# RWKV5 attention and an MLP-Mixer layer: `r` of 14 units is loaded with four consecutive tokens of two heads per partition

## The chip, the cores and the metric

The kernel runs on one core of one Trainium2 chip. The metric is the device time of one execution in microseconds; the number given for a kernel is the median of its runs.

## What is computed

Four sequences of 768 tokens, 8 heads of 48 channels. The attention keeps one 48 x 48 state per head, which decays by `w` per token:

```python
for t in range(S):
    kt, vt, rt = (k[:, :, t], v[:, :, t], r[:, :, t])
    cur = np.einsum('bhd,bhe->bhde', u[None] * kt, vt)
    y[:, :, t] = np.einsum('bhd,bhde->bhe', rt, state + cur)
    state = w[None, :, :, None] * state + np.einsum('bhd,bhe->bhde', kt, vt)
```

Its output, with the heads side by side as 384 channels, goes through a mixer layer. The token half mixes along the sequence, the channel half along the channels:

```python
xt = x.transpose(0, 2, 1)
h = np.maximum(xt @ w_tok1, 0.0) @ w_tok2
u = x + h.transpose(0, 2, 1)
h2 = np.maximum(u @ w_ch1, 0.0) @ w_ch2
return (u + h2)
```

All inputs and the output are float32 in DRAM; `r`, `k` and `v` are stored as (batch, head, token, channel), so 48 floats (192 bytes) of one head and token are contiguous, and so are consecutive tokens of one head.

## The kernel before

The 24 units of work are 4 batches times 6 chunks of 128 tokens, in that order. For each unit SyncE (SP) loads `k`, `r` and `v` into tiles `ld_k`, `ld_r`, `ld_v` of 128 partitions (one token each) by 8 heads by 48 channels. `lpool` holds eight units, so a load of unit u+8 waits until unit u has used its tile. The decay over time is taken out by products: `kp` multiplies `k` by a table `wn`, `rp` multiplies `r` by a table `wp`; both are powers of `w`, made at the start by ScalarE (ACT) as exp(t ln w), with t from `iota` and one table for each of G = 3 chunk positions. ln w comes from `w_ps`, in which a matmul of a column of ones has copied `w` to all partitions. The products go in bf16 to `kpr`, with each head padded to 64 columns, so that two heads fill 128.

`kpr` must then be turned, channels on partitions. For units 0 to 13 TensorE (PE) does it (`trk`, `trr`, into `tr_ps` in PSUM), and ACT copies the result to SBUF as `rk` (one copy of 1024 columns, or for the units in `rk_two` a copy of 512 for `k` and one for `r`: `rkk`, `rkr`). Units 14 to 23 (`turned`) are turned by a DMA transpose, `turn_unit`. From `rk` come the scores (`at_ps`), which VectorE (DVE) masks to `AT`; `y` adds the unit's own part and, through the state `S`, that of the units before; `yd` is the part of `u`; `x_b` is the attention's output. The mixer follows for each batch: `hid` (`wtok1`), `hr`, `bk` (`wtok2`), `us` (`u_sb`), `uT` (turned), then `z` (`wch1`), `zr`, `h` (`wch2`) and `os`, which is stored.

The order on each engine is fixed when the program is built. `graph` lists all steps with the engines that they may run on, their times and a rank; `Plan.run` simulates this and gives the order, and `InOrder` keeps it. The change doesn't touch `graph` or its numbers. Parts of it that the prediction speaks of:

- SP issues all loads and stores in one order, `transfers` at line 416, with a store or a transpose between them where it falls due. POOL (GpSimd) does most `kp` and `rp` products and issues the six weight transfers behind some of them (`wafter`, line 436): the two `wtok` after its products of unit 4, the four `wch` (two halves of `wch1`, two halves of `wch2`) after those of unit 5.
- `hold` lets the load of `k` for unit 6 wait until `y` of unit 5 is done.
- TensorE turns, scores and mixes in this one order too; while it waits early on, `fill` gives it idle matmuls.

Of the kernel before, what the change touches and what calls it, by code (L numbers as in the profile page):

```python
# [13 lines left out]
f32 = mybir.dt.float32  # L14
bf16 = mybir.dt.bfloat16
i32 = mybir.dt.int32
# [3 lines left out]
Exp = ACTF.Exp  # L20
Ln = ACTF.Ln

B, H, S, D = 4, 8, 768, 48
T = 128
C = S // T
G = C // 2
HP = H // 2
NJ = 12
NU = B * C
LEAD = 4  # L30
NLOAD = 8
LATER = tuple(range(2 * C, NU))

# [134 lines left out]
def graph(do, cfg):  # L168
# [49 lines left out]
    for u in range(NU):  # L218
# [4 lines left out]
        t_at, t_y, t_yS = cfg.get("pe_times", ((0.36, 0.25, 0.185),) * 2)[u >= C]  # L223
        old = xs.get(u - LEAD)
        d = cfg.get("dve_late", {}).get("kr", 0.5) if u >= cfg.get("early", 6) else cfg.get("kr0", 0.5)
# [189 lines left out]
CFG = dict(apart=2.0,   # L415
    transfers=[("u", u) for u in range(0, 6)]
    + [('k', 6)]
    + [('r', 6)]
    + [('k', 7)]
    + [('r', 7)]  # L420
    + [('v', 6)]
    + [('v', 7)]
    + [('u', 8)]
# [31 lines left out]
    late={'kp2': -0.6},  # L455
    hold={6: ('y', 5), 21: ('us', '2_2')},
    by_pe=range(0, 14),
    turned=range(14, 24),
    warm=(2, 4),
    fill_from=16.5,  # L460
# [5 lines left out]
def kernel(  # L466
# [13 lines left out]
    nc = tc.nc  # L480
    assert tuple(r.shape) == (B, H, S, D)
    dm = H * D
    MID = G * T // 2
# [2 lines left out]
    dch = moe_w_ch1.shape[1]  # L486
    by_pe = CFG.get("by_pe", range(NU))
    direct = CFG.get("direct", ())

    const = ctx.enter_context(tc.tile_pool(name="const", bufs=1))  # L490
    wts = ctx.enter_context(tc.tile_pool(name="wts", bufs=1))
    lpool = ctx.enter_context(tc.tile_pool(name="lpool", bufs=NLOAD))
    apool = ctx.enter_context(tc.tile_pool(name="apool", bufs=LEAD + 1))
    xpool = ctx.enter_context(tc.tile_pool(name="xpool", bufs=1))
# [3 lines left out]
    psM = ctx.enter_context(tc.tile_pool(name="psM", bufs=4, space=bass.MemoryType.PSUM))  # L498
# [19 lines left out]
    pe, dve, act, pool, sp = (InOrder(e) for e in (nc.tensor, nc.vector, nc.scalar, nc.gpsimd, nc.sync))  # L518
    ENG = {"PE": pe, "DVE": dve, "ACT": act, "POOL": pool, "SP": sp}

    def h3(t):
        return t.rearrange("p (h d) -> p h d", h=H)
# [2 lines left out]
    idle = const.tile([128, 512], bf16, name="idle")  # L525
    dve.memset(idle, 0.0)
    row = const.tile([1, dm], f32, name="row")
    rows = const.tile([2 * HP, 2, P], f32, name="rows")
    dve.memset(rows, 1.0)
    wide = len(by_pe) < NU  # L530
    u_bc = const.tile([128, dm], f32, name="u_bc") if wide else None
    act.dma_start(out=row, in_=w.rearrange("h d -> (h d)")[None, :])
    act.preload_act_table_set("natural_log_exp_and_others")
    ones = const.tile([1, 128], f32, name="ones")
    dve.memset(ones, 1.0)


    idle_ps = psM.tile([128, 512], f32, name="idle_ps", tag="m")
    w_ps = psM.tile([128, dm], f32, name="w_ps", tag="m")

    def warm(n):
        for _ in range(n):
            pe.matmul(idle_ps, idle[:, 0:128], idle, start=True, stop=True)

    warm(CFG.get("warm", (1, 10))[0])
    pe.matmul(w_ps, ones, row, start=True, stop=True)
    warm(CFG.get("warm", (1, 10))[1])

    iota_i = const.tile([128, 2, G], i32, name="iota_i")
# [1 line left out]
    pool.iota(iota_i[:, 1, :], pattern=[[-T, G]], base=MID - 1, channel_multiplier=-1)  # L551
    iota = const.tile([128, 2, G], f32, name="iota")
    dve.tensor_copy(iota, iota_i)
    ident = const.tile([128, 128], bf16, name="ident")
    make_identity(nc, ident)
    mask = const.tile([128, 128], f32, name="mask")
    pool.memset(mask, 1.0)
    pool.affine_select(
        out=mask, in_=mask, compare_op=ALU.is_gt,
# [12 lines left out]

    NB = LEAD + 1
    kprs = []
    for i in range(NB):
        t = const.tile([128, 2, H, P], bf16, name=f"kpr{i}")
# [16 lines left out]
    lnw = const.tile([128, dm], f32, name="lnw")  # L593
    wn = const.tile([128, G, dm], f32, name="wn")
    wp = const.tile([128, G, dm], f32, name="wp")
    wu_sb = const.tile([128, 2, HP], f32, name="wu_sb")
    wG = const.tile([128, HP], f32, name="wG")
    wGm = const.tile([128, HP, 2, D], f32, name="wGm")

    def lnw_(eng):  # L600
        act.activation(lnw, w_ps, Ln)

    def wn_(eng, g):
        act.activation(wn[:, g, :], lnw, Exp, scale=iota[:, 1, g:g + 1])

    def wp_(eng, g):
        act.activation(wp[:, g, :], lnw, Exp, scale=iota[:, 0, g:g + 1])

    def wu(eng):
# [20 lines left out]
    SRC = {"k": k, "r": r, "v": v}  # L630
    loaded, L, Z, M = {}, [dict() for _ in range(NU)], {}, [dict() for _ in range(B)]
    kvs, INS, M0 = [None, None], {}, {}

    def load(eng, nm, i):
        b, c = divmod(i, C)
        t = lpool.tile([128, dm], f32, name=f"ld_{nm}")
        ins = sp.dma_start(h3(t), SRC[nm][b, :, ts(c, T), :].rearrange("h s d -> s h d"))
        if i in CFG.get("hold", {}) and nm == "k":
            first = INS["".join(map(str, CFG["hold"][i]))]
            tc.add_manual_dep(ins.ins, first.ins.name,  # L640
                              mybir.DependencyInfo(mybir.DependencyClass.Sync, mybir.DependencyReason.DATA),
                              reason="weights first")
        loaded[nm, i] = t
# [15 lines left out]
        ENG[eng].tensor_mul(kprs[i % NB][:, 0, :, 0:D], h3(loaded["k", i]), h3(wn[:, i % G, :]))  # L659

    def rp(eng, i):
        ENG[eng].tensor_mul(kprs[i % NB][:, 1, :, 0:D], h3(loaded["r", i]), h3(wp[:, i % G, :]))

    def vb(eng, i):
        L[i]["vb"] = apool.tile([128, dm], bf16, name="vb")
        INS[f"vb{i}"] = act.copy(L[i]["vb"], loaded["v", i])

# [12 lines left out]
    def yd(eng, i):  # L680
        L[i]["yd"] = apool.tile([128, dm], f32, name="yd", bufs=LEAD)
        ENG[eng].tensor_mul(h3(L[i]["yd"]), h3(L[i]["vb"]), L[i]["adg"].unsqueeze(2).to_broadcast([128, H, D]))
# [12 lines left out]

    def rk(eng, i):
        L[i]["rk"] = apool.tile([128, 2, HP, T], bf16, name="rk")
        (act.copy if eng == "ACT" else dve.tensor_copy)(L[i]["rk"], L[i]["tr"])

    def rkp(eng, i, j):  # L700
        if "rk" not in L[i]:
            L[i]["rk"] = apool.tile([128, 2, HP, T], bf16, name="rk")
        (act.copy if eng == "ACT" else dve.tensor_copy)(L[i]["rk"][:, j], L[i]["tr"][:, j])

    def atq(eng, i, q):
        if q == 0:
# [20 lines left out]
    def AT(eng, i, q):  # L727
        if q is None:
# [267 lines left out]
```

## Time and profile before

| | |
|---|---|
| median of 3 runs | 166.17 us (164.99 to 168.54) |
| profiled execution, first to last instruction | 166.5 us |
| its own time, as given | the span is all that is given for it, 0.3 us above the median |
| TensorE matmul busy | 156.8 us (94%) |
| DVE, ACT, POOL busy | 106.8, 87.2, 65.3 us |
| read from and written to DRAM | 20.65 and 4.72 MB |
| DMA packets | 97427, of which 90753 under 512 bytes |

Times in the profile's rows count from the span's start, in us; a row of the timeline has start, duration, engine, line and operation, with output, inputs and shape, then the idle time ahead of it and what ended that. All engine instructions pass through one helper, so they show line L512 and are told apart by their tiles. "SPq" and "POOLq" are the issuing of DMAs. q1 is SP's queue, q10 ACT's, q0 POOL's.

### The profile page before, as it was taken

What the parts mean: (1) busy time and instruction counts of PE and PEld (TensorE: products, weight loads), DVE (VectorE), ACT (ScalarE), POOL (GpSimd) and SP (SyncE); (2) the same over time, 40 slices, a digit from 0 to 9 for tenths busy, and PEclk for the clock granted to TensorE, in tenths of its full rate; (3) what the DMA queues carried; (4) which work ended last, traced back from release to release, by engine and by line L of the source; (5) the groups of instructions that cost most, each with busy time, mean ns of one, the idle gap of its engine ahead of it and who ended that gap; (6) DMA issues with size and microseconds to landing.
All of it is one profiled execution on the core that took longest, in us unless ns stands there. A gap on an engine that the chain in (4) does not pass through costs nothing.

```text
span 166.5 us, 3791 instructions
## 1 busy us (share of the span) xinstructions
PE 156.8 (94%) x1462; PEld 100.6 (60%) x1464; DVE 106.8 (64%) x219; ACT 87.2 (52%) x182; POOL 65.3 (39%) x80
## 2 busy tenths in 40 slices
PE   6797999599999999999999999999999999999991
PEld 1377764356677666666666665666656655665671
DVE  5189996300459989899989889977885582021031
ACT  3996743279198636579804452069154502904900
POOL 7839970000009647386785857103840000000000
PEclk9999999789999999999999999999999999999999
DMA  5999999999699899999999994999990028012012
GB/s 100 215 213 210 159 187 176 188 184 168 131 208 287 158 192 216 217 230 182 198 192 169 230 158 106 188 235 222 171 240 6 4 50 218 16 51 94 0 47 94
DMA packets 97427, 26.26 MB, mean 158 GB/s; under 512 B 90753, under 2 KB 97410, under 8 KB 97410
## 3 DMA queue, kind: packets, MB, share of 16 engines
q1 hardware_dynamic: 93920, 22.88, 67.2%
q0 software_dynamic: 3488, 3.15, 12.3%
q8 instruction: 11, 0.18, 0.5%
q14 instruction: 6, 0.05, 0.1%
q10 hardware_dynamic: 2, 0.00, 0.0%
HBM read 20.65 MB, written 4.72 MB: 152 GB/s over the span
## 4 chain that ended last, share of the span: by engine, by line
PE 79%; DMA 8%; POOL 5%; ACT 3%; issue 2%; DVE 1%; SPq 1%; POOLq 0%
PE h_ps L512 31%; PE z_ps L512 29%; DMA wch<-in_moe_w_ch_dram 6%; PE y_ps L512 4%; PE at_ps L512 4%; PE hT_ps L512 3%; PE tr_ps L512 3%; POOL kpr L512 3%; PE kv_ps L512 2%; DMA ld_v<-in_v_dram 2%; PE t_ps L512 1%; ACT rk L512 1%; POOL wtok L512 1%; SPq L512 1%; POOL yd L512 0%
## 5 line engine op out<-in xcount | busy, mean ns | idle before, releaser
L512 ACT ACTIVATE zr<-z_ps 128x384 bf16<-128x384 f32 x94 | 45.5, 492 | 47.5 <-PE z_ps L512 47.3
L512 PE MATMUL z_ps<-uT,wch 128*128 128x384 bf16 x288 | 53.6, 331 | 2.0 <-DMA wch<-in_moe_w_ch_dram 2.0
L512 PE MATMUL h_ps<-wch,zr 128*128 128x384 bf16 (+1 forms) x300 | 52.5, 319 | 0.0
L512 PEld LDWEIGHTS <-wch 128*128 128x128 bf16 x288 | 27.0, 99 | 18.8 <-DMA wch<-in_moe_w_ch_dram 2.4
L512 PEld LDWEIGHTS <-zr 128*128 128x128 bf16 x300 | 27.9, 98 | 15.5 <-issue 0.2
L512 POOL TENSOR_TENSOR yd<-vb,adg 128x384 f32<-128x384 bf16 x18 | 15.5, 860 | 46.5 <-ACT adg L512 27.9
L512 DVE TENSOR_TENSOR AT<-at_ps,mask 128x512 bf16<-128x512 f32 x43 | 27.9, 682 | 0.7 <-PE at_ps L512 0.6
L512 DVE TENSOR_TENSOR osb<-u_sb,h_ps 128x384 f32<-128x384 bf16 (+1 forms) x22 | 11.7, 533 | 23.4 <-PE h_ps L512 23.3
L512 POOL TENSOR_TENSOR kpr<-ld_r,wp 128x384 bf16<-128x384 f32 x16 | 16.6, 1036 | 5.3 <-ACT wp L512 2.8
L512 ACT COPY rk<-tr_ps 128x512 bf16<-128x512 bf16 (+1 forms) x20 | 15.0, 756 | 4.9 <-PE tr_ps L512 4.5
L512 PEld LDWEIGHTS <-kpr 128*128 128x128 bf16 x192 | 13.7, 107 | 6.0 <-POOL kpr L512 2.6
L512 DVE TENSOR_TENSOR x_b<-y_ps,yd 128x384 bf16<-128x384 f32 x24 | 13.2, 552 | 5.2 <-PE y_ps L512 5.1
L512 POOL TENSOR_TENSOR kpr<-ld_k,wn 128x384 bf16<-128x384 f32 x15 | 15.2, 1011 | 1.8 <-DMA ld_r<-in_r_dram 0.7
L512 PEld LDWEIGHTS <-rk 48*128 48x128 bf16 (+1 forms) x272 | 11.0, 99 | 6.4 <-issue 2.7
L512 ACT CAST vb<-ld_v 128x384 bf16<-128x384 f32 x24 | 12.3, 511 | 4.3 <-POOL kpr L512 3.1
L512 PE MATMUL tr_ps<-ident,kpr 128*128 128x128 bf16 x112 | 12.1, 245 | 2.4 <-ACT rk L512 1.4
L512 DVE TENSOR_TENSOR S<-kv_ps,bm 128x384 bf16<-128x384 f32 x13 | 7.2, 551 | 6.0 <-PE kv_ps L512 5.8
L512 DVE TENSOR_TENSOR u_sb<-x_b,hT_ps 128x384 bf16<-128x384 bf16 x21 | 10.4, 546 | 0.9 <-PE hT_ps L512 0.9
L512 PEld LDWEIGHTS <-wtok 128*128 128x128 bf16 x90 | 8.0, 98 | 4.8 <-issue 0.6
L512 PEld LDWEIGHTS <-AT 128*128 128x128 bf16 x192 | 8.4, 98 | 3.4 <-DVE AT L512 0.8
L512 PE MATMUL at_ps<-rk 48*128 48x128 bf16 x192 | 10.2, 229 | 0.2 <-ACT rk L512 0.2
L512 PE MATMUL h_ps<-x_b,wtok 128*128 128x384 bf16 x48 | 10.2, 326 | 0.0
(81 smaller groups left out, 145.4 us busy)
## 6 DMA issues: line engine op xcount, KB each, us to landing
ld_k<-in_k_dram SPq DMA_DIRECT2D x24, 192.0 KB, 3.8
ld_r<-in_r_dram SPq DMA_DIRECT2D x24, 192.0 KB, 3.8
ld_v<-in_v_dram SPq DMA_DIRECT2D x24, 192.0 KB, 3.8
out_dram<-osb SPq DMA_DIRECT2D x23, 192.0 KB, 2.6
wch<-in_moe_w_ch_dram POOLq DMA_DIRECT2D x4, 576.0 KB, 14.2
wtok<-in_moe_w_tok_dram POOLq DMA_DIRECT2D x2, 384.0 KB, 6.4
u_bc<-in_u_dram SPq DMA_DIRECT2D x1, 192.0 KB, 5.0
out_dram<-osb SPq DMA_DIRECT2D x2, 96.0 KB, 1.6
```

What stands on the lines that cost most here:

```text
L512: ins = tc.keep_in_program_order(f(*args, **kw))
```

## The change

`r` of the units in `split` (0 to 13, those that TensorE turns) is loaded in another layout. Partition 32 a + s now holds four consecutive tokens 4s to 4s+3 of the two heads 2a and 2a+1. In DRAM four tokens of one head are 192 floats (768 bytes) in one piece. A load is two DMAs, one for each head of the pairs (q). In the tile the columns are (q, j, channel), j being the token of the four.

The table `wp` is made to fit: token and head now change with the partition. A second small load, `row4`, holds `w` with two heads per partition; a second matmul into `w_ps` with a 4 x 128 matrix `quarter` gives each partition the `w` of its two heads, ACT takes the logarithm (`lnr`), DVE multiplies it by the tokens (`iota_r`) into `wp`, and ACT takes the exponential in place. `rp` puts the product to `kpr` in the order (j, q), so that the four blocks that TensorE turns are the four j. The block of j then has the columns (a, s). The copy `rk` of the `r` half puts token 4s+j of head pair a in its place, with strided reads of PSUM; since the `k` half is as before, all 14 units have two copies now. Units 14 to 23 read `r` as before, so `vb` of units 13, 14 and 15 first makes `wp` of one chunk position in the old form (`wp_as_read`).

```diff
+R = HP
...
+    split=range(0, 14),
...
+    row4 = const.tile([HP, 2 * D], f32, name="row4")
...
     act.dma_start(out=row, in_=w.rearrange("h d -> (h d)")[None, :])
+    act.dma_start(out=row4, in_=w.rearrange("(a q) d -> a (q d)", q=2))
...
-    w_ps = psM.tile([128, dm], f32, name="w_ps", tag="m")
+    w_ps = psM.tile([128, dm + 2 * D], f32, name="w_ps", tag="m")
...
-    pe.matmul(w_ps, ones, row, start=True, stop=True)
+    pe.matmul(w_ps[:, 0:dm], ones, row, start=True, stop=True, skip_group_check=True)
+    ident = const.tile([128, 128], bf16, name="ident")
+    make_identity(nc, ident)
+    quarter = const.tile([HP, HP, T // R], f32, name="quarter")
+    dve.tensor_copy(quarter, ident[0:HP, 0:HP].unsqueeze(2).to_broadcast([HP, HP, T // R]))
+    pe.matmul(w_ps[:, dm:], quarter.rearrange("p a t -> p (a t)"), row4, start=False, stop=True, skip_group_check=True)
...
-    ident = const.tile([128, 128], bf16, name="ident")
-    make_identity(nc, ident)
+    iota_ri = const.tile([128, G, R], i32, name="iota_ri")
+    for a in range(HP):
+        pool.iota(iota_ri[a * (T // R):(a + 1) * (T // R)], pattern=[[T, G], [1, R]], base=-MID, channel_multiplier=R)
+    iota_r = const.tile([128, G, R], f32, name="iota_r")
+    dve.tensor_copy(iota_r, iota_ri)
...
     def lnw_(eng):
-        act.activation(lnw, w_ps, Ln)
+        act.activation(lnr.rearrange("p q d -> p (q d)"), w_ps[:, dm:], Ln)
+        act.activation(lnw, w_ps[:, 0:dm], Ln)
+        shape = [128, 2, R, D]
+        for g in range(G):
+            dve.tensor_mul(wr[:, g], lnr.unsqueeze(2).to_broadcast(shape), iota_r[:, g].unsqueeze(1).unsqueeze(3).to_broadcast(shape))
...
     def wp_(eng, g):
+        act.activation(wp[:, g, :], wp[:, g, :], Exp)
+
+    def wp_as_read(g):
+        natural.add(g)
         act.activation(wp[:, g, :], lnw, Exp, scale=iota[:, 0, g:g + 1])
...
-        ins = sp.dma_start(h3(t), SRC[nm][b, :, ts(c, T), :].rearrange("h s d -> s h d"))
+        src = SRC[nm][b, :, ts(c, T), :]
+        if nm == "r" and i in split:
+            for q in range(2):
+                ins = sp.dma_start(t[:, ts(q, dm // 2)], src.rearrange("(a q) (s j) d -> q a s (j d)", q=2, j=R)[q])
+        else:
+            ins = sp.dma_start(h3(t), src.rearrange("h s d -> s h d"))
...
-        ENG[eng].tensor_mul(kprs[i % NB][:, 1, :, 0:D], h3(loaded["r", i]), h3(wp[:, i % G, :]))
+        if i in split:
+            ENG[eng].tensor_mul(kprs[i % NB][:, 1, :, 0:D].rearrange("p (j q) d -> p q j d", q=2),
+                                loaded["r", i].rearrange("p (q j d) -> p q j d", q=2, j=R), wr[:, i % G])
+        else:
+            ENG[eng].tensor_mul(kprs[i % NB][:, 1, :, 0:D], h3(loaded["r", i]), h3(wp[:, i % G, :]))
...
     def vb(eng, i):
+        if i + 1 not in split and len(natural) < G:
+            wp_as_read((i + 1) % G)
...
     def rk(eng, i):
+        if i in split:
+            for j in range(2):
+                rkp(eng, i, j)
...
     def rkp(eng, i, j):
-        (act.copy if eng == "ACT" else dve.tensor_copy)(L[i]["rk"][:, j], L[i]["tr"][:, j])
+        to, src = L[i]["rk"][:, j], L[i]["tr"][:, j]
+        if j == 1 and i in split:
+            to, src = to.rearrange("p a (t j) -> p a t j", j=R), src.rearrange("p j (a t) -> p a t j", a=HP)
+        (act.copy if eng == "ACT" else dve.tensor_copy)(to, src)
```

On SP the program begins with the loads of units 0 and 1 (the shape is that of the tile's side). Before:

```order
L512 DMA ld_k<-in_k_dram 128x8x48
L512 DMA ld_r<-in_r_dram 128x8x48
L512 DMA ld_v<-in_v_dram 128x8x48
L512 DMA ld_k<-in_k_dram 128x8x48
L512 DMA ld_r<-in_r_dram 128x8x48
L512 DMA ld_v<-in_v_dram 128x8x48
```

And now, with the line of the same helper three further down:

```order
L515 DMA ld_k<-in_k_dram 128x8x48
L515 DMA ld_r<-in_r_dram 128x1x192 x2
L515 DMA ld_v<-in_v_dram 128x8x48
L515 DMA ld_k<-in_k_dram 128x8x48
L515 DMA ld_r<-in_r_dram 128x1x192 x2
L515 DMA ld_v<-in_v_dram 128x8x48
```

Each load of `r` is two DMAs of 128 rows of 192 floats; nothing has changed places.

On POOL the weight transfers stand among the products of units 4 and 5 (`kpr_138` and `kpr_130` are the two units' buffers), now:

```order
L515 TENSOR_TENSOR kpr_138<-ld_k,wn 128x8x48
L515 DMA wtok_159<-in_moe_w_tok_dram 128x6x256
L515 TENSOR_TENSOR kpr_138<-ld_r,wp 128x2x4x48
L515 DMA wtok_160<-in_moe_w_tok_dram 128x2x768
L515 TENSOR_TENSOR kpr_130<-ld_k,wn 128x8x48
L515 TENSOR_TENSOR kpr_130<-ld_r,wp 128x2x4x48
L515 DMA wch_161<-in_moe_w_ch_dram 128x3x768 x2
L515 DMA wch_162<-in_moe_w_ch_dram 128x6x384 x2
```

The same rows stood there before, with other buffer numbers and the shape 128x8x48 for the `r` products: no weight transfer has moved past a product.

On ACT the start is longer. Before:

```order
L512 DMA row<-in_w_dram 1x384
L512 ACT_TABLE_LOAD
L512 ACTIVATE lnw<-w_ps 128x384
L512 ACTIVATE wn<-lnw,iota 128x384
L512 ACTIVATE wp<-lnw,iota 128x384
L512 CAST vb<-ld_v 128x384
```

And now:

```order
L515 DMA row<-in_w_dram 1x384
L515 DMA row_85<-in_w_dram 4x96
L515 ACT_TABLE_LOAD
L515 ACTIVATE lnr<-w_ps 128x96
L515 ACTIVATE lnw<-w_ps 128x384
L515 ACTIVATE wn<-lnw,iota 128x384
L515 ACTIVATE wp<-wp 128x384
L515 CAST vb<-ld_v 128x384
```

The second DMA (`row4`) and the logarithm of 96 columns have come in ahead of `lnw`, and with it ahead of every table.

More of the change, by code (lines that the diff above doesn't have):

```diff
@@ L488 @@
     direct = CFG.get("direct", ())
+    split = CFG.get("split", ())
     const = ctx.enter_context(tc.tile_pool(name="const", bufs=1))
@@ L595 @@
     wp = const.tile([128, G, dm], f32, name="wp")
+    wr = wp.rearrange("p g (q j d) -> p g q j d", q=2, j=R)
+    lnr = const.tile([128, 2, D], f32, name="lnr")
+    natural = set()
     wu_sb = const.tile([128, 2, HP], f32, name="wu_sb")
@@ L661, in rp @@
     def rp(eng, i):
-        ENG[eng].tensor_mul(kprs[i % NB][:, 1, :, 0:D], h3(loaded["r", i]), h3(wp[:, i % G, :]))
+        assert (i % G in natural) == (i not in split)
+        if i in split:
[3 more added lines that the diff above has]
+            ENG[eng].tensor_mul(kprs[i % NB][:, 1, :, 0:D], h3(loaded["r", i]), h3(wp[:, i % G, :]))
     def vb(eng, i):
+        if i + 1 not in split and len(natural) < G:
+            wp_as_read((i + 1) % G)
         L[i]["vb"] = apool.tile([128, dm], bf16, name="vb")
@@ L697, in rk @@
         L[i]["rk"] = apool.tile([128, 2, HP, T], bf16, name="rk")
-        (act.copy if eng == "ACT" else dve.tensor_copy)(L[i]["rk"], L[i]["tr"])
+        if i in split:
+            for j in range(2):
+                rkp(eng, i, j)
+        else:
+            (act.copy if eng == "ACT" else dve.tensor_copy)(L[i]["rk"], L[i]["tr"])
     def rkp(eng, i, j):
```

## The prediction

> **What bounds the kernel now.** I read the page's shares first, then the chain that ended last in order of time, then windows and the queues.
>
> ```profile
> PE 156.8 (94%) x1462; PEld 100.6 (60%) x1464; DVE 106.8 (64%) x219; ACT 87.2 (52%) x182; POOL 65.3 (39%) x80
> ...
> 20.86 10.02 DMA wch<-in_moe_w_ch_dram
> ...
> 30.92 0.85 PE z_ps L512 x3
> ```
>
> TensorE is busy for 94%, so from the first MLP product on the kernel lasts as long as its matmuls. What can still be won or lost lies ahead of that product, which started at 30.92 us: 166.5 - 30.92 = 135.6 us follow it. The chain says that it waited for the first half of `wch1`, whose transfer was issued at 20.86 us. The windows show the price of that wait:
>
> ```profile
> 2.00:16.00 14.00, 11.88 (x105) 7.78 (x105) 8.62 (x27) 11.71 (x25) 10.05 (x14) 1.00 1.07 211
> 28.00:31.00 3.00, 0.98 (x7) 0.40 (x6) 1.90 (x4) 0.11 (x1) 0.00 (x0) 1.00 1.17 202
> 31.00:36.00 5.00, 5.00 (x27) 3.03 (x28) 0.72 (x2) 2.65 (x6) 0.00 (x0) 0.66 1.26 184
> ```
>
> The last three columns are granted clock, DMA share and GB/s. TensorE did 0.98 us of work in 28 to 31, and afterwards ran at a clock of 0.66 for five microseconds. The DMA engines are saturated all the while (share 1.07 to 1.26). From 2 to 16 us they carry the token loads and next to nothing else: 211 GB/s x 14 us = 2.95 MB, or 15.0 loads of 192 KB, one per 0.93 us. What issues `wch` is POOL, in its own order, behind its last product of unit 5:
>
> ```profile
> 18.95 1.01 POOL L512 TENSOR_TENSOR kpr<-ld_k,wn 128x384 bf16<-128x384 f32 x1
> 19.91 0.99 POOL L512 TENSOR_TENSOR kpr<-ld_r,wp 128x384 bf16<-128x384 f32 x1
> 20.86 3.26 POOL L512 DMA_DIRECT2D wch<-in_moe_w_ch_dram  x4
> ...
> 15.12 0.75 SPq L512 DMA_DIRECT2D ld_r<-in_r_dram  x1
> ...
> ld_r<-in_r_dram SPq DMA_DIRECT2D x24, 192.0 KB, 3.8
> ```
>
> `r` of unit 5 was issued at 15.12 and lands a median 3.8 us later, at 18.9; its product starts at 19.91. So the load is hidden with 1.0 us to spare. If `r` comes later than that, everything behind `wch` moves with it.
>
> **The load that changes.** First the price of one packet, of 192 bytes (4 to 16 us) and of 768 bytes (the last two stores, 128 rows of 192 floats each):
>
> ```profile
> DMA packets 288, 0.20 MB, mean 61 GB/s; under 512 B 32, under 2 KB 288, under 8 KB 288
> ...
> q1 hardware_dynamic: 288, 0.20, 19.5%
> ...
> q1 hardware_dynamic: 13527, 2.56, 108.0%
> ...
> q10 hardware_dynamic: 2, 0.00, 0.0%
> ```
>
> The third row gives 1.080 x 12 us x 16 engines / 13,527 = 15.3 ns for 192 bytes. The second, over 3.2 us, gives 0.195 x 3.2 x 16 = 10.0 us for 256 data packets and 32 short ones, about 38 ns for 768 bytes. A load of `r` goes from 1,024 packets of 192 bytes to 256 of 768: 15.7 to 9.7 us of engine time in all. Spread over 16 engines that is 0.98 to 0.61 us, a gain of 0.37 us.
>
> How far it spreads is what decides. The two stores have an outermost dimension of 128 rows on both sides and end with 32 short packets, 16 each: one completion per engine. The load of `row` has an outermost dimension of 1, and its queue (q10) holds two packets, one of data and one completion: one engine. The new loads have 128 partitions on the SBUF side, but on the DRAM side an outermost dimension of 4 (`a`, then 32 runs of 768 bytes). No row shows that shape. The ends are 16 engines and 1. I read the `row` load as saying that the smaller outer count limits the spread, and here that is 4: so I take four engines, the same four for both halves, which differ in nothing but an offset. Then each of them gets 2 x 32 packets x 38 ns = 2.43 us for one load of `r`, where every engine had 64 x 15.3 = 0.98. Packets overlap a little (0.98 us of them pass in 0.93), so the difference counts as (2.43 - 0.98) x 0.95 = **1.4 us per load of `r`**.
>
> The Trainium skill, "DMA: Bandwidth & Descriptors", section "Why a DMA increments its semaphore by 16 and not by 1", states the step between: the number of engines is the largest number up to 16 that divides the slowest dimension of both access patterns, and the hardware queues take the lowest-numbered ones. By it 4 and 128 give four engines, 0 to 3, for both halves; the one-row load agrees (2 packets), and no run here shows a count of 4. By it the sum stands as below; if the 128 partitions alone counted, it would be the first rival's.
>
> **The sum, up to the first MLP product.** Units 0 to 5 have six such loads in one queue with the `k` and `v` loads, which use the same four engines too: `r` of unit 5 lands 6 x 1.4 = 8.4 us later, at 27.3. On top come the two `wtok` transfers:
>
> ```profile
> wtok<-in_moe_w_tok_dram POOLq DMA_DIRECT2D x2, 384.0 KB, 6.4
> ...
> q0 software_dynamic: 3424, 3.15, 68.0%
> ```
>
> The second row is the window 15 to 45 us, with all six weight transfers: 0.68 x 30 = 20.4 us on each engine. The two `wtok` are 768 of 3,072 KB, so 5.1 us. POOL issues them behind its products of unit 4, and so far they came when the loads were nearly done. With the loads of units 4 and 5 still queued on four engines they share with them: 0 to 5.1 us, and I take 4, since only the last unit's tail can escape them. `r` of unit 5 then lands at 31.3, its product ends at 32.3, and `wch` is issued 11.4 us later than 20.86. Between the end of unit 5's product (20.90) and the end of the last work ahead of the MLP,
>
> ```profile
> 27.76 1.14 PE L512 MATMUL hT_ps<-h1r,wtok 128*128 128x384 bf16 x6
> ```
>
> at 28.90, lie 8.0 us of transposes, scores, hidden layer and back; so TensorE is ready at 40.3. The first `wch` landed 10.0 us after its issue, with `wtok` and the last load ahead of it; its own part of the 20.4 us is 576/3,072, or 3.8. Issued at 32.3 it lands between 36.1 and 42.3, and only what is later than 40.3 counts: I take 40.9. The first MLP product moves from 30.92 to there: **+10.0 us**. Its ends: +6.6 (packets 10% cheaper, no sharing) and +13 (all of `wtok` shared, `wch` in 10 us again).
>
> **Units 6 to 13.** Their eight `r` loads add 8 x 1.4 = 11.2 us on the four engines. What is there to swallow it:
>
> ```profile
> 44.46 0.84 SPq L512 DMA_DIRECT2D ld_r<-in_r_dram  x1
> ...
> 60.97 0.73 SPq L512 DMA_DIRECT2D ld_r<-in_r_dram  x1
> ...
> 50.67 1.08 POOL L512 TENSOR_TENSOR kpr<-ld_r,wp 128x384 bf16<-128x384 f32 x1 [0.25 <-PE at_ps L512]
> ...
> 67.67 1.00 POOL L512 TENSOR_TENSOR kpr<-ld_r,wp 128x384 bf16<-128x384 f32 x1 [0.55 <-PE kv_ps L512]
> ...
> q1 hardware_dynamic: 29315, 6.73, 99.0%
> ```
>
> These are `r` of units 8 and 13, issue and use: with 3.8 us to land they are 2.4 and 2.9 us early. The last row is 43 to 75 us: packets fill 99.0%, against 108.0% where the queue is full, which leaves 0.09/1.08 of the 25 us up to 68, 2.1 us. The loads of units 6 and 7 run beside the weights. There the second half of `wch2` has room:
>
> ```profile
> L512 POOL DMA_DIRECT2D wch<-in_moe_w_ch_dram x4: 775/818/861, 20.9 to 23.3; - x4
> ...
> DMA to landing us min/median/max: 10.0/14.2/19.0
> ...
> 44.86 1.14 PE L512 MATMUL h_ps<-wch,zr 128*128 128x384 bf16 x6
> ```
>
> Issued last, at 23.3, it lands 19.0 us later at 42.3, and is first used at 44.86: 2.5 us. 11.2 - 2.9 - 2.1 - 2.5 = 3.7; I take **+4 us**, with ends 0 (the other work hides it) and 8.3 (only the 2.9 is there). SP waits in order behind full queues, so stores and the later loads come late with it; from unit 14 on the loads are the old ones and the lag is worked off.
>
> **What else is edited.** The start gets a second small DMA on ACT, a matmul of 96 columns (some 0.4 us, a quarter of the 1.64 below), a logarithm over 96 columns (between 0.21 and 0.49 us), three DVE products (beside ACT) and four small iotas on POOL.
>
> ```profile
> 2.23 1.64 PE L512 MATMUL w_ps<-row,ones 1*128 1x384 f32 x2
> 3.91 0.49 ACT L512 ACTIVATE lnw<-w_ps 128x384 f32<-128x384 f32 x1 [1.28 <-PE w_ps L512]
> ...
> 9.83 0.21 ACT L512 ACTIVATE wG<-wu_sb 128x4 f32<-128x4 f32 x1
> ...
> 11.12 0.63 ACT L512 ACTIVATE wp<-lnw,iota 128x384 f32<-128x384 f32 x1
> 11.82 1.00 POOL L512 TENSOR_TENSOR kpr<-ld_r,wp 128x384 bf16<-128x384 f32 x1 [2.77 <-ACT wp L512]
> ```
>
> ACT is 11.71 of 14 us busy from 2 to 16, and POOL waited 2.77 us for its `wp`; it starts 0.4 + 0.3 = 0.7 us later. The late loads cover that from unit 1 on; without them it is +0.7. `rk` of units 5 and 7 to 13 becomes two copies:
>
> ```profile
> 21.49 1.01 ACT L512 COPY rk<-tr_ps 128x1024 bf16<-128x1024 bf16 x1 [1.29 <-PE tr_ps L512]
> ...
> 19.07 0.59 ACT L512 COPY rk<-tr_ps 128x512 bf16<-128x512 bf16 x1
> ```
>
> 2 x 0.59 - 1.01 = 0.17 us more each, 1.4 in all on an engine that is busy for 52%. That 14 of the copies read PSUM with a stride is shown nowhere: 0 to as much again (0.59); the nearest row is the contiguous copy, so 0. The `r` products keep runs of 48 floats: 0. Three more exponentials (0.63 us each) ahead of `vb` 13 to 15 lie beside TensorE's MLP work. SP issues 14 more DMAs, of 0.4 to 0.8 us each as the rows above have them, 8 us in all; it stands before full queues most of that time, so I count none of it.
>
> 166.5 + 10.0 + 4 = **180.5 us**. That is against the profiled span of 166.5, which is 0.3 us above the median 166.17; I say 180.
>
> **The rivals.** *Sixteen engines (not slower).* If the DRAM side's 4 doesn't count, six loads save 6 x 0.37 = 2.2 us. POOL's order still sets when `wch` is issued, 0.7 us later by the start, but nothing is ahead of it then. TensorE is ready at 29.6 instead of waiting to 30.92, and without the idle 2 us the clock may hold (0.34 x 5 us = 1.7 us of work in 31 to 36). That is 0.7 to 3.0 us off, about 164.5. For it speaks that everything up to 40 us is bound by DMA; against it, the single engine of `row`. The Trainium skill, same page, "Specifications", asks for 512 bytes and more per descriptor for line rate; the trace agrees in kind, 38 ns for four times the bytes of 15.3, and by that rule alone this rival's 164.5 would be the time.
>
> *Eight engines.* The halves fall on two different sets of four: each has 1.22 us where it had 0.98, 0.24 x 6 = 1.4 us plus 0.7 of the start, about 168.5. Against it: two DMAs of one shape, alike but for an offset.
>
> *Four engines, but prefetch hides units 6 to 13*: 176; *or nothing hides them*: 187. Both lie in the main case.
>
> **How the numbers follow.** Four engines: 0.80, with its own range 173 to 189 (166.5 + 6.6 + 0, and 166.5 + 13 + 8.3 = 187.8, a little more for stores that come late). Sixteen: 0.12. Eight: 0.08. The sixteen are left out; 170 to 190 holds nearly all of the main case. Within 2% (3.3 us) is about what a measurement tells from no change: faster by more than that only in the best of the sixteen, 0.04; within, 0.13; slower, 0.83.
>
> **What would show it.** In the changed profile: `ld_r` takes longer to land than `ld_k` did (well over 3.8 us); the DMA share falls far below 1.07 in 2 to 16 us while loads are waited for; POOL's products wait for `ld_r`; `wch` is issued near 32 us; TensorE idles ahead of that, and between 45 and 85 waits for products of units 8 to 13. A DMA share that stays at 1, with more bytes per second than 211, and `wch` issued at 21 to 22 us would prove the step on engines wrong.

## The result: 180.3 us, 9.1% slower, and the profile after

The changed kernel takes 180.31 us (median of 4 runs, 180.00 to 181.33), the kernel before beside it 165.88 us (164.99 to 168.54): a ratio of 1.0909, 95% interval 1.0864 to 1.0954. The forecast was 180. The profiled execution took 180.39 us, of which 178.7 lie between its first and last instruction. That gap of about 1.7 us is in every run that gives both numbers, and it matters further down. Ratios, here and in the table further down, leave out executions in which the core was disturbed, while medians hold them, which shows only in the run with eight engines.

The page of the changed kernel, first the shares, then queues, chain and loads:

```profile
PE 160.0 (90%) x1464; PEld 103.0 (58%) x1466; DVE 110.7 (62%) x224; ACT 89.0 (50%) x194; POOL 66.7 (37%) x84
...
q1 hardware_dynamic: 83056, 22.88, 58.7%
...
q10 hardware_dynamic: 10, 0.00, 0.0%
...
PE 68%; SPq 14%; DMA 8%; ACT 3%; POOL 2%; issue 1%; DVE 1%; POOLq 0%; ACTq 0%
...
ld_k<-in_k_dram SPq DMA_DIRECT2D x24, 192.0 KB, 4.6
...
ld_r<-in_r_dram SPq DMA_DIRECT2D x28, 96.0 KB
```

TensorE is busy 3.2 us longer, but its share has fallen from 94% to 90% of a longer span. SP's issuing and the DMAs of `ld_r` are now 22% of the chain that ended last.

The packet counts show the number of engines. A completion is the short packet beyond the data, one for each engine in the two stores and the `row` load that the prediction read. The queue q10 carries the two small loads of `w`: `row`, one data packet and one completion as before, and `row4`, whose outermost count is 4. 10 - 2 = 8 packets for it are four of data and four completions. In q1 the 28 half loads have 28 x 128 data packets; the rest of the queue, 93,920 before less 14 old `r` loads of 1,024 + 16, is 79,360. 83,056 - 79,360 - 3,584 = 112 = 28 x 4 completions. Four engines end each half load; sixteen would have made 83,392.

The windows (busy us of PE, PEld, DVE, ACT, POOL, then clock, DMA share, GB/s), first the one with the early loads, then the stretch in which units 8 to 13 are done:

```profile
2.00:16.00 14.00, 9.88 (x71) 5.94 (x70) 7.68 (x26) 9.48 (x22) 7.12 (x13) 1.00 0.64 138
...
60.00:65.00 5.00, 4.15 (x59) 3.04 (x57) 4.29 (x10) 4.06 (x9) 3.64 (x4) 1.00 0.86 230
65.00:70.00 5.00, 4.26 (x60) 2.89 (x59) 4.54 (x8) 0.79 (x3) 2.29 (x3) 1.00 0.58 131
70.00:75.00 5.00, 3.71 (x45) 2.41 (x43) 3.19 (x7) 2.71 (x7) 2.86 (x4) 1.00 0.65 144
75.00:80.00 5.00, 4.05 (x59) 2.74 (x58) 3.52 (x7) 2.77 (x7) 2.61 (x3) 1.00 0.73 172
80.00:90.00 10.00, 9.11 (x105) 6.21 (x103) 8.60 (x19) 7.69 (x19) 6.54 (x7) 1.00 1.02 232
```

From 2 to 16 us, where the loads had filled the DMA engines (share 1.07, 211 GB/s), they now stand at 0.64 and 138 GB/s while the loads are waited for. From 60 to 90 us TensorE is idle for 30 - 25.28 = 4.7 us (0.5 in the same 30 us before). The window from 2 to 16 us once more, cut into 40 slices of 0.35 us, in tenths of all sixteen engines:

```profile
DMA  6993016379589933422377799953330369799943
```

Again and again the share sinks to 2 or 3 tenths: 4 of 16 engines is 0.25. It isn't `r` alone that passes then. From 8.3 to 9.0 us the share is 0.26 and 54 of 92 packets are over 512 bytes, so those of `r`. From 11.5 to 12.1 us it is 0.32 and all 207 packets are under 512 bytes, so those of `k` and `v`. The completions in the trace tell why: of the sixteen of the `ld_v` that was issued at 7.77 us, twelve came from 10.05 to 11.34, the last four from 11.84 to 12.04; in the run with sixteen engines further down all sixteen of the `ld_v` issued at 7.80 us came from 10.17 to 10.83. So four engines, busy with `r` before that, still had their part of `v` to do.

POOL's rows show who waits, and the end of the wait:

```profile
11.73 1.00 POOL L515 TENSOR_TENSOR kpr<-ld_r,wp 128x384 bf16<-128x384 f32 x1 [1.59 <-DMA ld_r<-in_r_dram]
...
24.42 0.99 POOL L515 TENSOR_TENSOR kpr<-ld_r,wp 128x384 bf16<-128x384 f32 x1 [1.32 <-DMA ld_r<-in_r_dram]
25.37 0.78 POOL L515 DMA_DIRECT2D wtok<-in_moe_w_tok_dram  x1
26.17 1.02 POOL L515 TENSOR_TENSOR kpr<-ld_k,wn 128x384 bf16<-128x384 f32 x1
30.10 1.00 POOL L515 TENSOR_TENSOR kpr<-ld_r,wp 128x384 bf16<-128x384 f32 x1 [2.91 <-DMA ld_r<-in_r_dram]
31.03 3.26 POOL L515 DMA_DIRECT2D wch<-in_moe_w_ch_dram  x4
```

The product of unit 5 starts at 30.10 instead of 19.91, and `wch` is issued at 31.03 instead of 20.86. The first MLP product follows:

```profile
39.13 1.14 PE L515 MATMUL hT_ps<-h1r,wtok 128*128 128x384 bf16 x6
40.11 0.65 PE L515 MATMUL z_ps<-uT,wch 128*128 128x384 bf16 x3
```

It starts at 40.11 (30.92 before), with no wait for `wch`: TensorE comes straight from the work of units 0 to 5.

### The profile page after: what moved, and what is told of

It is laid out like the page before. It is cut to its first block, busy times and chain, and to the rows that moved or that the text cites. A ratio compares the mean times of both kernels' runs of the same rounds, so it can differ in the third digit from the quotient of the medians.

```text
span 178.7 us, 3849 instructions
## 1 busy us (share of the span) xinstructions
PE 160.0 (90%) x1464; PEld 103.0 (58%) x1466; DVE 110.7 (62%) x224; ACT 89.0 (50%) x194; POOL 66.7 (37%) x84
## 3 DMA queue, kind: packets, MB, share of 16 engines
q1 hardware_dynamic: 83056, 22.88, 58.7%
## 4 chain that ended last, share of the span: by engine, by line
PE 68%; SPq 14%; DMA 8%; ACT 3%; POOL 2%; issue 1%; DVE 1%; POOLq 0%; ACTq 0%
PE h_ps L515 29%; PE z_ps L515 26%; SPq L515 14%; DMA ld_r<-in_r_dram 8%; PE at_ps L515 4%; PE y_ps L515 3%; PE hT_ps L515 3%; POOL kpr L515 2%; PE kv_ps L515 2%; PE tr_ps L515 1%; ACT rk L515 1%; POOL yd L515 1%; ACT wp L515 1%; PE t_ps L515 1%; ACT vb L515 1%
## 5 line engine op out<-in xcount | busy, mean ns | idle before, releaser
L515 PE MATMUL z_ps<-uT,wch 128*128 128x384 bf16 x288 | 52.4, 326 | 0.1
L515 PE MATMUL tr_ps<-ident,kpr 128*128 128x128 bf16 x112 | 13.1, 254 | 12.6 <-POOL kpr L515 9.2
L515 ACT COPY rk<-tr_ps 128x512 bf16<-128x512 bf16 x28 | 15.5, 587 | 10.9 <-PE tr_ps L515 10.7
L515 ACT CAST vb<-ld_v 128x384 bf16<-128x384 f32 x24 | 12.2, 510 | 12.3 <-DMA ld_v<-in_v_dram 12.3
L515 PEld LDWEIGHTS <-rk 48*128 48x128 bf16 (+1 forms) x272 | 11.8, 104 | 6.5 <-issue 3.3
L515 PE MATMUL h_ps<-x_b,wtok 128*128 128x384 bf16 x48 | 11.4, 355 | 0.0
L515 PE MATMUL at_ps<-rk 48*128 48x128 bf16 x192 | 10.8, 240 | 0.4 <-ACT rk L515 0.2
L515 DVE TENSOR_TENSOR kpr<-ld_k,wn 128x384 bf16<-128x384 f32 x9 | 6.4, 709 | 6.3 <-DMA ld_k<-in_k_dram 6.1
## 6 DMA issues: line engine op xcount, KB each, us to landing
wch<-in_moe_w_ch_dram POOLq DMA_DIRECT2D x4, 576.0 KB, 10.9
```

What stands on the lines that cost most here:

```text
L515: ins = tc.keep_in_program_order(f(*args, **kw))
```

## The experiments

Three theories were set against each other. **A**: the outermost count of 4 on the DRAM side puts a load on four engines, and that is the whole loss. **B**: something else in the new layout costs it (packets of 768 bytes, strided copies out of PSUM, the longer start). **C**: two DMAs for a load cost it, since SP issues them in order.

All results in one table; "first z" is the start of the first MLP product in the profiled execution, "behind it" the span less that. The ratio is to the kernel before in the same comparison.

| kernel | median us | ratio, 95% interval | span | first z | behind it |
|---|---|---|---|---|---|
| before, profile of the prediction | 166.17 | | 166.5 | 30.92 | 135.6 |
| changed | 180.31 | 1.0909 (1.0864 to 1.0954) | 178.7 | 40.11 | 138.6 |
| sixteen engines | 165.64 | 1.0021 (0.9998 to 1.0043) | 164.9 | 30.81 | 134.1 |
| eight engines | 168.59 | 1.0162 (1.0084 to 1.0241) | 165.6 | 31.58 | 134.0 |
| two engines | 211.48 | 1.2809 (1.2749 to 1.2868) | 209.1 | 55.54 | 153.6 |
| four only for units 0 to 5 | 176.09 | 1.0639 (1.0599 to 1.0678) | 174.4 | 40.34 | 134.1 |
| before, four-engine loads alone | 179.59 | 1.0843 (1.0795 to 1.0891) | 178.2 | 41.06 | 137.1 |
| before, two DMAs of 192-byte packets | 167.63 | 1.0112 (1.0053 to 1.0171) | 166.4 | 32.72 | 133.7 |
| whole layout, one DMA, sixteen engines | 166.06 | 1.0064 (1.0028 to 1.0099) | 165.6 | 31.19 | 134.4 |
| before, with those loads alone | 165.57 | 1.0031 (1.0011 to 1.0051) | 163.7 | 29.41 | 134.3 |
| whole layout, one `wch` earlier | 165.88 | 1.0046 (1.0031 to 1.0062) | 164.2 | 29.74 | 134.5 |
| before, one `wch` earlier | 165.18 | 1.0007 (0.9992 to 1.0023) | 163.4 | 29.08 | 134.3 |
| whole layout, weights earlier | 172.57 | 1.0446 (1.0402 to 1.0489) | 170.9 | 36.55 | 134.4 |
| before, weights earlier | 172.19 | 1.0421 (1.0377 to 1.0465) | 170.5 | 36.34 | 134.2 |

**Sixteen engines, everything else as changed.** The rows come from a region whose outermost count is 128:

```diff
-    ... src.rearrange("(a q) (s j) d -> q a s (j d)", q=2, j=R)[q]
+    flat = r[b].rearrange("h s d -> (h s d)")[ts(c, T * dm)].rearrange("(p q x) -> q p x", p=128, q=2)
+    ... flat[q]
```

> The changed kernel, except that each half of an r load reads 128 rows of 768 bytes whose DRAM side also has an outermost count of 128 (every second row of one contiguous region, so other tokens than those asked for). Same two DMAs, same 256 packets of 768 bytes, same tables, products and copies. Theory A (the outer count of 4 puts the load on four engines): all that was lost comes back, 163.5 to 167.5 us; the first MLP product starts at 30 to 32 us, the DMA share in 2 to 16 us is near 1, POOL does not wait for ld_r in units 1 to 5, q1 has 83,056 + 28 x 12 = 83,392 packets. Theory B (the 768-byte packets, the strided copies out of PSUM or the longer start cost it): 178 to 182. Theory C (two DMAs for each load, issued in order by SP): most of the loss stays, 174 to 182.

Measured: 165.64 us, 1.0021 of before. All of the loss is gone, with the two DMAs, the packets, the tables and the copies still there. The page and the window 2 to 16 us of this kernel:

```profile
q1 hardware_dynamic: 83392, 22.88, 64.2%
...
ld_r<-in_r_dram SPq DMA_DIRECT2D x28, 96.0 KB, 3.2
```
```profile
2.00:16.00 14.00, 11.74 (x99) 8.08 (x100) 9.98 (x32) 11.65 (x26) 10.29 (x17) 1.00 1.03 225
```

The count is the one for sixteen completions, the share is back at 1.03 and the bytes per second above the old 211. B falls, and with packets of 768 bytes C does too.

**Eight engines.** Same bytes, packets and DMAs:

```diff
+    ... src[:, ts(q, T // 2), :].rearrange("h (s j) d -> h s (j d)", j=R)
```

> The changed kernel, except that each half of an r load reads 64 tokens of all eight heads (8 x 16 rows of 768 bytes), so its DRAM side has an outermost count of 8; tokens and heads stand in other partitions than the tables have. Same bytes, same packets, same number of DMAs. Theory A: eight engines, each with 2 x 16 x 38 ns = 1.22 us for one load where it was 0.98 before the change: 0.24 x 6 = 1.4 us on units 0 to 5 and some 0.7 for the start, 166 to 170 us, q1 83,056 + 28 x 4 = 83,168 packets. Theories B and C: no difference to the changed kernel, 178 to 182.

Measured: 1.0162 of before, which on its 165.33 us is 168.0. That is 2.7 us more (1.4 to 4.0 by the interval), where 1.4 for six loads and 0.7 for the start were expected. The count again names the engines, and the share lies between the other two:

```profile
q1 hardware_dynamic: 83168, 22.88, 63.5%
```
```profile
2.00:16.00 14.00, 11.25 (x90) 7.66 (x90) 9.48 (x30) 11.24 (x25) 9.84 (x16) 1.00 0.87 190
```

**Two engines.** Each half reads 256 tokens of two heads:

```diff
+    ... r[b, 2 * q:2 * q + 2, lo:lo + 2 * T, :].rearrange("h (s j) d -> h s (j d)", j=R)
```

> The changed kernel, except that each half of an r load reads 256 tokens of two heads (2 x 64 rows of 768 bytes), so its DRAM side has an outermost count of 2; the tile holds other tokens than the tables have. Same bytes, packets and number of DMAs. Theory A: two engines, each with 2 x 64 x 38 ns = 4.9 us for one load of r, 2.4 us more than with four: 14 x 4.9 = 68 us of loads in units 0 to 13, of which the first six push the MLP back by 6 x 2.4 = 14.6 us more than in the changed kernel and the next eight by up to 19 more: 200 to 215 us; q1 83,056 - 28 x 4 = 82,944 packets. If four engines were a floor or the cost lay elsewhere: 178 to 184.

Measured: 211.48 us. The first MLP product comes 15.4 us later than with four engines (55.54 against 40.11), against 14.6 by packets times 38 ns; behind it another 15.0 us are lost, in part at a lower granted clock (0.89 from 60 to 90 us, 1.00 with four engines).

```profile
q1 hardware_dynamic: 83000, 22.88, 49.2%
```
```profile
2.00:16.00 14.00, 7.35 (x35) 3.84 (x34) 4.51 (x19) 5.63 (x11) 6.11 (x12) 1.00 0.44 96
```

The expected count had a slip (two completions fewer for each half is 28 x 2 below 83,056, not 28 x 4). With it mended, 2, 4, 8 and 16 engines give 83,000, 83,056, 83,168 and 83,392: always 82,944 and 28 times the number of engines. The Trainium skill, "DMA: Bandwidth & Descriptors", "Why a DMA increments its semaphore by 16 and not by 1", states that the engines are the largest number up to 16 that divides the slowest dimension of both sides; at 2, 4, 8 and 16 the traces agree. That the lower-numbered ones are taken no run here shows.

**Four engines for units 0 to 5 only**, sixteen for 6 to 13:

```diff
+    ... four[q] if i < 6 else flat[q]
```

> The changed kernel, except that the r loads of units 6 to 13 read rows with an outermost count of 128 (other tokens). Units 0 to 5 are as in the changed kernel. Theory A: the first MLP product stays near 40 us, the 4.7 us of TensorE idle in 60 to 80 us go: 173 to 176.5. If the idle there is set by something else, 179 to 181.

Measured: 176.09 us, 4.2 less than the changed kernel. The first MLP product stays where it was (40.34), and what goes is the idle time behind it:

```profile
60.00:65.00 5.00, 5.00 (x74) 3.71 (x73) 4.62 (x12) 4.55 (x11) 3.82 (x5) 1.00 1.01 225
65.00:70.00 5.00, 5.00 (x63) 3.16 (x60) 4.30 (x9) 1.83 (x5) 3.45 (x4) 1.00 0.84 214
70.00:75.00 5.00, 5.00 (x86) 3.76 (x83) 4.79 (x10) 3.22 (x10) 3.73 (x4) 1.00 0.81 195
75.00:80.00 5.00, 4.53 (x52) 2.81 (x50) 4.40 (x10) 3.30 (x9) 2.60 (x3) 1.00 0.96 192
80.00:90.00 10.00, 9.72 (x95) 6.41 (x95) 9.37 (x18) 9.07 (x22) 7.17 (x8) 1.00 1.17 210
```

29.25 of 30 us are busy, where 25.28 were. So 4.2 us of the loss belong to the loads of units 6 to 13, and the rest to the late first six units; the reverse, four engines for the later loads alone, was not run.

**The kernel before, with nothing but the four-engine loads:**

```diff
+        if nm == "r" and i < 14:
+            for q in range(2):
+                ins = sp.dma_start(t[:, ts(q, dm // 2)], src.rearrange("(a q) (s j) d -> q a s (j d)", q=2, j=4)[q])
```

> The kernel before, with nothing of the change but the r loads of units 0 to 13: its tables and products take the tile as if it were in the old order, so what it computes with r is not the reference's. Theory A: the loads alone cost all of it, 177 to 181 us, first MLP product at 38 to 41. Theory B (start, tables, strided copies): no more than 168. Theory C (two DMAs) would give the same as A here, and is told apart by the run with sixteen engines.

Measured: 179.59 us. The loads alone cost 8.4% of the change's 9.1% (the intervals overlap). What is left for start, tables and second copies is 0.7 us at the medians, 1.1 by the ratios. B falls from this side too.

**Two DMAs of the old form**, 192-byte packets on sixteen engines:

```diff
+            for q in range(2):
+                ins = sp.dma_start(h3(t)[:, ts(q, HP)], src[:, ts(q, HP)])
```

> The kernel before, except that r of units 0 to 13 is loaded by two DMAs of four heads each, in the old layout (192-byte packets, DRAM side outermost 128). It computes the reference. Theory A (SP's 14 more issues lie before full queues): 164.5 to 167.5. Theory C (two DMAs per load cost SP time that the loads need): 14 x 0.75 us of issue, of which 6 ahead of the MLP show, 168 to 172.

Measured: 1.0112 of before. The median of 167.63 us lies between the two expectations. Here two DMAs do cost something, 1.9 us on 165.16. SP's rows for the last `r` load ahead of the MLP, first in this kernel, then in the one with sixteen engines and 768 bytes:

```profile
15.08 2.92 SPq L512 DMA_DIRECT2D ld_r<-in_r_dram  x2
18.05 0.51 SPq L512 DMA_DIRECT2D ld_v<-in_v_dram  x1
```
```profile
13.95 1.37 SPq L515 DMA_DIRECT2D ld_r<-in_r_dram  x2
15.37 0.43 SPq L515 DMA_DIRECT2D ld_v<-in_v_dram  x1
```

With small packets SP is held, its last load is issued 2.7 us later than there (2.1 later than in the kernel before), and POOL waits 2.69 us for `r` of unit 5; with large ones it doesn't. So C is a small effect of its own with packets of 192 bytes, and nothing measurable with those of the change.

**The whole layout on sixteen engines, with one DMA.** The partition order is turned round, 4s + a instead of 32a + s; tables and copy are made to fit:

```diff
-    ... src.rearrange("(a q) (s j) d -> q a s (j d)", q=2, j=R)[q]
+    ins = sp.dma_start(t, src.rearrange("h (s j) d -> s h (j d)", j=R))
...
-        to, src = to.rearrange("p a (t j) -> p a t j", j=R), src.rearrange("p j (a t) -> p a t j", a=HP)
+        to, src = to.rearrange("p a (t j) -> p a t j", j=R), src.rearrange("p j (t a) -> p a t j", a=HP)
```

> The changed kernel with the partition order turned round: partition 4s + a (not 32a + s) holds tokens 4s to 4s+3 of heads 2a and 2a+1. Tables, quarter, iota_r and the strided copy are made to fit, so it computes the reference. On the DRAM side the outermost count is now 32 (s), then 8 heads, then 768 bytes, and one DMA does a whole load of r. Theory A (the four engines were the whole loss): 163.5 to 167, as the run with sixteen engines (165.6) or a little less for half the DMAs; nothing of the 14 us remains. Theory B (products, copies, or the layout of partitions cost something of their own): above 168.

Measured: 166.06 us, 1.0064 of before. That undoes the loss by an order of dimensions, but there is no gain. This load reads the same bytes of `r` as the changed kernel's, which the runs with sixteen and eight engines don't: so where the bytes lie in DRAM isn't the cause either.

**Why no gain: the same loads in the kernel before**, without the longer start and the second copies:

```diff
+            ins = sp.dma_start(t, src.rearrange("h (s j) d -> s h (j d)", j=4))
```

> The kernel before, with nothing of the change but r of units 0 to 13 loaded by one DMA in the turned-round partition order (768-byte packets, DRAM side outermost 32, sixteen engines); tables and products take the tile as in the old order, so what is computed with r is not the reference's. It holds the wide loads without the longer start and without the second copies. If those cost what the 166.06 against 165.16 of the full version suggests, this one is 0.5 to 1.0 us below that version and about as fast as before or a little faster, 164.3 to 165.5; wch is then issued near 20.9 instead of 21.6. If the wide loads themselves cost something, it is at 166 as well.

Measured: 165.57 us, just above what was expected, 1.0031 of before. It is 0.5 us below the full version, which would be the price of the start and the copies (the two intervals overlap); the loads themselves bring nothing, though they end sooner. POOL's rows show why a sooner load is of no use:

```profile
14.50 1.25 POOL L512 TENSOR_TENSOR kpr<-ld_r,wp 128x384 bf16<-128x384 f32 x1 [0.36 <-DVE AT L512]
15.70 1.00 POOL L512 TENSOR_TENSOR kpr<-ld_k,wn 128x384 bf16<-128x384 f32 x1
16.64 0.89 POOL L512 DMA_DIRECT2D wtok<-in_moe_w_tok_dram  x1
...
20.26 1.01 POOL L512 TENSOR_TENSOR kpr<-ld_r,wp 128x384 bf16<-128x384 f32 x1
21.20 3.25 POOL L512 DMA_DIRECT2D wch<-in_moe_w_ch_dram  x4
```

Behind the short wait for `AT` at 14.50 POOL has no idle time before any product until 21.2: its own order, 1 us a product, sets when `wch` is issued, 0.3 us later than before. In this profile the 0.3 us arise at the start: ACT's first `vb` waits 0.42 us for `ld_v` and begins at 5.97 (5.61 before), and ACT hands the delay on to the `wp` for which POOL waits (its product begins at 12.19, 11.82 before). That would fit the 0.3%, as far as one profile of each kernel tells.

**One `wch` transfer ahead of POOL's products of unit 5**, in the whole layout and, as a control, in the kernel before; no other instruction changes its place:

```diff
+    first = next(n for n, s in enumerate(steps) if s.name == "kp5")
+    steps.insert(first, steps.pop(next(n for n, s in enumerate(steps) if s.name == "i:w2")))
```

> The whole layout with one DMA, and POOL issues the first half of wch1 right ahead of its two products of unit 5 instead of behind them; no other instruction changes its place on any engine. wch is issued at 19.7 instead of 21.6; the two products and all behind them come 0.8 us later, so TensorE is ready at about 29.7. If the issue sets the landing, the first MLP product starts at 29.7 to 30.3 instead of 31.2: 164.5 to 165.5. If the DMA engines do (wtok and the loads ahead of wch), it stays at 31: 166 to 166.8.

> The kernel before, with the same one transfer moved. Its loads of 192-byte packets last to 19 us, so wch shares the engines with the last of them: if the issue sets the landing 164 to 165.3, if the engines do 165.5 to 167.

Measured: 165.88 and 165.18 us. TensorE's wait for `wch` is gone from both profiles. In the whole layout the first MLP product came at 29.74, where the issue was to put it, and yet the time stayed above the 164.5 to 165.5 expected with it: its ratio, 1.0046, isn't apart from the 1.0064 without the move (the intervals overlap). The control is as fast as before (1.0007, 0.9992 to 1.0023). So the wait that the prediction read in the profile before, 2.02 us, seems to belong to that execution. Its span of 166.5 us would be 168.2 us with the 1.7 around it, 2.0 us above the median of 166.17 and not 0.3, near the slowest of the three times given; the control's 163.4 (165.09 us) is a usual one. The mean granted clock of that profile was 0.990, that of 55 later executions of the kernel before 0.996 or more. And the wait was 1.06 us in two profiles of other versions that took 166.61 and 167.31 us, and 0.28 us in one that took 165.41 us. In a usual execution the move is worth no more than 0.1%; that it also puts the two products 0.8 us later may offset a part.

**Weights earlier by a new plan**, in the whole layout and in the kernel before (wtok about units 3 and 4):

```diff
-    wafter={0: 'x:r4', 1: 'x:r4', 2: 'rp5', 4: 'kp5', 3: 'rp5', 5: 'rp5'},
+    wafter={0: 'x:r3', 1: 'x:r3', 2: 'rp4', 4: 'kp5', 3: 'rp5', 5: 'rp5'},
```

> The same kernel as the whole layout with one DMA, and beside it the six weight transfers are issued earlier on POOL: wtok about units 3 and 4, the first half of wch1 ahead of the two products of unit 5, the other three behind them. If, with the 768-byte packets on sixteen engines, the wait of TensorE for wch ahead of the first MLP product (1.1 us of idle in 28 to 31 us in the run with sixteen engines) is set by when POOL issues it, the product moves 1 to 2 us ahead: 163 to 165 us. If the queues are full then and wch only pushes the loads back, 165 to 168.

> The kernel before, with the same earlier issue of the weights and nothing else. There the 192-byte loads fill the queues to 19 us, so the weights push the loads of units 4 and 5 back: 165 to 168.5. If it is as fast as the one with 768-byte packets, the gain, if any, is that of the weights' order alone.

Measured: 172.57 and 172.19 us, out of both ranges. These two say little on the loads: the planner, given other issue times, also put the transposes of unit 5 (`tr_ps`) later on TensorE, behind idle matmuls (`fill_ps`), as the timeline of the first of them shows. POOL had done its products of unit 5 by 22.64 us:

```profile
26.55 2.32 PE L515 MATMUL fill_ps<-idle 128*128 128x512 bf16 x10
28.70 0.39 PE L515 MATMUL tr_ps<-ident,kpr 128*128 128x128 bf16 x4
28.93 0.70 PE L515 MATMUL fill_ps<-idle 128*128 128x512 bf16 x3
29.47 0.39 PE L515 MATMUL tr_ps<-ident,kpr 128*128 128x128 bf16 x4
29.69 1.14 PE L515 MATMUL fill_ps<-idle 128*128 128x512 bf16 x5
```

That is why the transfer alone was moved, above. No version here beats the kernel before.

## Why the prediction was right, step by step

The mechanism was right: four engines, 1.4 us for each load, and both parts of the loss. That 180 met 180.31 so closely is in part luck: the terms up to the first MLP product were off by more than a microsecond in both directions, and the sum started from a span and not from a time.

**Four engines, from an outermost count of 4.** Right. It was inferred from one row, two packets for a load with an outermost count of 1; the counts at 2, 4, 8 and 16 now show it, and the times follow.

**1.4 us for each load.** Right. The issue of `ld_v`, which ends each unit on SP, shows the pace. Before, with the loads running full, and changed:

```profile
4.65 0.78 SPq L512 DMA_DIRECT2D ld_v<-in_v_dram  x1
...
15.92 1.71 SPq L512 DMA_DIRECT2D ld_v<-in_v_dram  x1
```
```profile
7.77 0.48 SPq L515 DMA_DIRECT2D ld_v<-in_v_dram  x1
...
21.78 2.63 SPq L515 DMA_DIRECT2D ld_r<-in_r_dram  x2
24.45 0.48 SPq L515 DMA_DIRECT2D ld_v<-in_v_dram  x1
```

Four units took 11.27 us, 2.82 each, and now 16.68, 4.17 each: 1.35 us more. It shows as issue time because SP is held at the first half of each load: of the pair's 2.63 us that half takes 2.06 (21.78 in the chain below), where the same pair on sixteen engines took 1.37 in all.

**4 us of sharing with `wtok`.** Too much. `r` of unit 5 is used at 30.10, where it was to land at 31.3; its last half was issued 8.8 us later than the old load (23.89, from the chain below, against 15.12) and landed 6.0 us after that, 2.2 more than the usual 3.8:

```profile
21.78 2.06 SPq L515
...
23.89 5.99 DMA ld_r<-in_r_dram
...
30.10 1.01 POOL kpr L515
31.15 0.41 PE tr_ps L515 x4
...
40.27 0.50 PE z_ps L515 x3
```

So the term is 2.2 us at most. The same halves of units 1 to 4, with less or nothing of `wtok` beside them, landed 4.4 to 4.6 us after their issue by the trace's completions. Against them sharing cost 1.4 to 1.6 us.

**8.0 us of work up to the MLP, then a wait for `wch` to 40.9.** Three errors that nearly cancel, which is luck. The product of unit 5 ended at 31.10 and not at 32.3, 1.2 us sooner; the way from there to the first `z` is 9.2 us on the chain, 1.2 more; and no wait for `wch`, forecast at 0.6 us, follows it. 40.1 was measured, 40.9 forecast.

**4 us for units 6 to 13.** Right: 4.7 us of idle in 60 to 90 us where 0.5 were, and 4.2 us of time when those loads are spread. More than half of the 11.2 us of added engine time is swallowed, as forecast; which of the three items of that sum swallowed how much, no run separates.

**Start 0.7 us, hidden.** Neither is shown by the times: the versions with and without start and second copies differ by 0.7 us with the late loads and 0.5 without, both from intervals that overlap. For hidden speaks that with the late loads the version that lacks the start comes to its first `z` no sooner (41.06, against 40.11 of the changed kernel). It gains behind it (137.1 against 138.6 us), where the changed kernel's second copies and three more exponentials stand.

**Against which time.** This step failed, unnoticed. The sum was made on the span of 166.5 us and read as if it were a time. The change of span is 178.7 - 166.5 = 12.2, not 14: 9.2 up to the first `z`, 3.0 behind it. There TensorE is idle for 7.8 us instead of 3.9, and its matmuls take 130.8 instead of 131.7: the profile before has a dip of the clock to 0.66 in 31 to 36 us, which in the changed kernel falls ahead of the MLP. The missing 1.8 us were made up, by luck, by the 1.7 us that lie around every span. Against a usual execution of before (165.09 us, span 163.4), with the 134.2 us behind the first `z` that the kernels without late loads have in the table, its first `z` would be at 29.2, an estimate, and the two parts are 40.1 - 29.2 = 10.9 and 138.6 - 134.2 = 4.4 us. They sum to 15.3. The medians give 14.4, and 15.0 to 15.2 against the later medians of the kernel before, 165.33 to 165.12.

**The rival with sixteen engines, 164.5.** With sixteen engines the time is that of before, not 0.7 to 3.0 us less. What failed in it, as far as the run with the earlier `wch` tells, is the step that took the 2 us of waiting for `wch`, and the dip of the clock behind it, as there in every execution. The Trainium skill's rule in "Specifications", 512 bytes and more per descriptor, agrees in kind with the queue (225 GB/s instead of 211 from 2 to 16 us, and 10,528 packets fewer in the run with sixteen engines). The time didn't follow: POOL's order and not the loads sets when `wch` is issued there, and an earlier issue gained nothing in the kernel before either.

## What to carry to other kernels

When a load is rearranged for longer runs, look at the outermost count on both sides before looking at the bytes in a run: at 4 these loads left 12 of 16 DMA engines without work, and the same bytes with 32 outermost cost 0.6% in the whole layout and 0.3% alone. The completions in the packet count of SP's queue told the number of engines from a profile, without a timing. And before a wait in a profiled execution is priced, compare that execution's own time, not its span, with the usual ones: removing a wait of 2 us there gained nothing in the median.

## What the runs showed of the hardware that was not expected

- With four engines SP is held while issuing: from the second load on a pair of half loads took 2.57 to 2.87 us of SP's time up to unit 5, with sixteen engines 1.0 to 1.7. So `k` and `v`, which use all engines, were issued late as well, and four of their sixteen completions came later than the rest, by 0.5 us and more: `vb` waited 12.3 us for `ld_v` in ten places of the changed kernel.
- Two DMAs of 96 KB in 192-byte packets cost 1.1% over one of 192 KB (1.0053 to 1.0171), in 768-byte packets nothing that could be measured (0.9998 to 1.0043).
- The copy of `rk` that reads PSUM with a stride takes as long as the contiguous one: the 28 copies of the changed kernel, of which 14 are strided, took 563 to 606 ns, and the contiguous ones of 512 columns before 586 ns in the mean.
